# A GEGLU feed-forward block on one core: warm-up matmuls, a new order of the first loads, and eight PSUM banks shared out anew

## The chip, the core and the metric

The kernel runs on one core of a Trainium2 chip. The metric is the device time of one execution in microseconds (us); the time before is the median of five runs.

## What is computed

```python
B, S, D, F = 32, 32, 1024, 3584          # x: B x S x D, weights D x F, D x F, F x D, all bf16

def _gelu(x):
    return jax.nn.gelu(x, approximate=True)

def reference(x, w_gate, w_up, w_down):
    return (_gelu(x @ w_gate) * (x @ w_up)) @ w_down
```

With 32 x 32 = 1024 rows of x, the two projections into F and the one back take 448 matmuls of 128 x 128 weights by 512 columns each, 1344 in all.

## The kernel before

All of x is held transposed in `xT` (128 partitions, DK = 8 slices of D, 1024 columns of tokens). It is filled by two DMA transposes at line 72, one for each block of 512 tokens (`tb` = 0, 1). All of the intermediate result lies in `GT` and all of `w_down` in `Wd`.

**First phase** (lines 91 to 141). An outer loop over seven groups `g` of 512 columns of F loads a tile `wg` of `w_gate` and a tile `wu` of `w_up`, 1 MB each, from a pool of two buffers (so the next group's load can go out while this one is used). In group 0 each of the two loads is split: columns 0 to 127 first (line 79), the other 384 after that (line 82). Behind them comes a chunk of `Wd` (line 97). Inside, for each of the two token blocks and each of four sub-blocks `fsub` of 128 columns, eight matmuls accumulate into a PSUM tile `pg` (line 108), eight into `pu` (line 117), and an element-wise chain follows: Square on ACT (line 125, out `s2`, which the profile calls `s`), a multiply-add on DVE (`inner`, line 127), Sigmoid on ACT (`sg`, line 136), and two multiplies on DVE (`t1`, shown as `t`, line 138; and `GT`, line 139, which is the only step that reads `pu`).

**Second phase** (lines 150 to 165). For each of 16 output tiles 28 matmuls accumulate into `po` (line 154); ACT copies it to SBUF (line 162), and SP sends it out (line 163).

PSUM has eight banks, and each of these tiles takes one: `pg` has three buffers, `pu` three, `po` two. PE, ACT, DVE and SP each run their own instructions in program order; a tile scheduler sets that order and the semaphores. All DMAs are issued by SP's queue, so a transfer that stands later in that queue is issued after the descriptors of all before it have been generated.

Of the kernel before, what the change touches and what calls it, by code (L numbers as in the profile page):

```python
# [1 line left out]

# [4 lines left out]


@with_exitstack  # L10
def kernel(
    ctx: ExitStack,
    tc: tile.TileContext,
    x: bass.AP,
    w_gate: bass.AP,
    w_up: bass.AP,
    w_down: bass.AP,
    out: bass.AP,
):
    nc = tc.nc  # L20
    P = nc.NUM_PARTITIONS

    bf16 = mybir.dt.bfloat16
    f32 = mybir.dt.float32
    ACT = mybir.ActivationFunctionType
    ALU = mybir.AluOpType

    xf = x.flatten_outer_dims()
    of = out.flatten_outer_dims()
    T, D = xf.shape  # L30
    D2, F = w_gate.shape
    assert D2 == D and w_up.shape == (D, F) and w_down.shape == (F, D)
    assert T % P == 0 and D % P == 0 and F % P == 0

    NB = 512
    DK = D // P
    FK = F // P
    TB = T // NB
    DN = D // NB
    TI = T // P  # L40
    FG = NB
    assert F % FG == 0 and T % NB == 0 and D % NB == 0
    NFG = F // FG
    FSUB = FG // P

    k_cubic = 0.044715
    sqrt_k = k_cubic**0.5
    sig_scale = 2.0 * (2.0 / 3.141592653589793) ** 0.5

    wg_v = w_gate.rearrange("(dk p) f -> p dk f", p=P)  # L50
    wu_v = w_up.rearrange("(dk p) f -> p dk f", p=P)
    wd_v = w_down.rearrange("(fk p) d -> p fk d", p=P)

    const_pool = ctx.enter_context(tc.tile_pool(name="consts", bufs=1))
    w_pool = ctx.enter_context(tc.tile_pool(name="wpool", bufs=2))
    work_pool = ctx.enter_context(tc.tile_pool(name="work", bufs=3))
    o_pool = ctx.enter_context(tc.tile_pool(name="opool", bufs=3))
    psum1_pool = ctx.enter_context(tc.tile_pool(name="psum1", bufs=3, space=bass.MemoryType.PSUM))
    psum2_pool = ctx.enter_context(tc.tile_pool(name="psum2", bufs=2, space=bass.MemoryType.PSUM))

    hwdge = [nc.sync, nc.sync]
    ldeng = nc.sync

    xT = const_pool.tile([P, DK, T], bf16, name="xT")
    GT = const_pool.tile([P, FK, T], bf16, name="GT")
    Wd = const_pool.tile([P, FK, D], bf16, name="Wd")
    WD_CHUNK = 4
    assert FK % WD_CHUNK == 0
    NWDC = FK // WD_CHUNK

    for tb in range(TB):
        nc.sync.dma_start_transpose(  # L72
            out=xT[:, :, tb * NB : (tb + 1) * NB],
            in_=xf[tb * NB : (tb + 1) * NB, :],
        )

    def load_w(tile_ap, dram_view, g, split_first):
        if split_first:
            ldeng.dma_start(
                out=tile_ap[:, :, 0:P], in_=dram_view[:, :, g * FG : g * FG + P]  # L80
            )
            ldeng.dma_start(
                out=tile_ap[:, :, P:FG],
                in_=dram_view[:, :, g * FG + P : (g + 1) * FG],
            )
        else:
            ldeng.dma_start(out=tile_ap, in_=dram_view[:, :, g * FG : (g + 1) * FG])

    wd_loaded = [False] * NWDC

    for g in range(NFG):
        wg = w_pool.tile([P, DK, FG], bf16, name="wg")
        load_w(wg, wg_v, g, split_first=(g == 0))
        wu = w_pool.tile([P, DK, FG], bf16, name="wu")
        load_w(wu, wu_v, g, split_first=(g == 0))
        if g < NWDC:
            ldeng.dma_start(
                out=Wd[:, g * WD_CHUNK : (g + 1) * WD_CHUNK, :],
                in_=wd_v[:, g * WD_CHUNK : (g + 1) * WD_CHUNK, :],
            )  # L100
            wd_loaded[g] = True
        for tb in range(TB):
            tsl = slice(tb * NB, (tb + 1) * NB)
            for fsub in range(FSUB):
                fi = g * FSUB + fsub
                pg = psum1_pool.tile([P, NB], f32, name="pg")
                for dk in range(DK):
                    nc.tensor.matmul(  # L108
                        pg,
                        lhsT=wg[:, dk, fsub * P : (fsub + 1) * P],  # L110
                        rhs=xT[:, dk, tsl],
                        start=(dk == 0),
                        stop=(dk == DK - 1),
                    )
                pu = psum1_pool.tile([P, NB], f32, name="pu")
                for dk in range(DK):
                    nc.tensor.matmul(  # L117
                        pu,
                        lhsT=wu[:, dk, fsub * P : (fsub + 1) * P],
                        rhs=xT[:, dk, tsl],  # L120
                        start=(dk == 0),
                        stop=(dk == DK - 1),
                    )
                s2 = work_pool.tile([P, NB], f32, name="s2")
                nc.scalar.activation(s2, pg, ACT.Square, scale=sqrt_k)  # L125
                inner = work_pool.tile([P, NB], f32, name="inner")
                nc.vector.scalar_tensor_tensor(  # L127
                    out=inner,
                    in0=s2,
                    scalar=1.0,  # L130
                    in1=pg,
                    op0=ALU.add,
                    op1=ALU.mult,
                )
                sg = work_pool.tile([P, NB], f32, name="sg")
                nc.scalar.activation(sg, inner, ACT.Sigmoid, scale=sig_scale)  # L136
                t1 = work_pool.tile([P, NB], f32, name="t1")
                nc.vector.tensor_tensor(out=t1, in0=sg, in1=pg, op=ALU.mult)  # L138
                nc.vector.tensor_tensor(  # L139
                    out=GT[:, fi, tsl], in0=t1, in1=pu, op=ALU.mult  # L140
                )

    for c in range(NWDC):
        if not wd_loaded[c]:
            ldeng.dma_start(
                out=Wd[:, c * WD_CHUNK : (c + 1) * WD_CHUNK, :],
                in_=wd_v[:, c * WD_CHUNK : (c + 1) * WD_CHUNK, :],
            )

    for ti in range(TI):  # L150
        for dn in range(DN):
            po = psum2_pool.tile([P, NB], f32, name="po")
            for fk in range(FK):
                nc.tensor.matmul(  # L154
                    po,
                    lhsT=GT[:, fk, ti * P : (ti + 1) * P],
                    rhs=Wd[:, fk, dn * NB : (dn + 1) * NB],
                    start=(fk == 0),
                    stop=(fk == FK - 1),
                )  # L160
            o_sb = o_pool.tile([P, NB], bf16, name="o_sb")
            nc.scalar.activation(o_sb, po, ACT.Copy)  # L162
            nc.sync.dma_start(
                out=of[ti * P : (ti + 1) * P, dn * NB : (dn + 1) * NB], in_=o_sb
            )


# [1 line left out]
_INS = ['x', 'w_gate', 'w_up', 'w_down']  # L169
_OUTS = [((32, 32, 1024), 'bfloat16')]  # L170


# [23 lines left out]
```

## Time and profile before

| | us |
|---|---|
| median of five runs (310.3 to 311.23) | 310.96 |
| the profiled execution's own time | 311.1 |
| its span, first to last instruction | 309.3 |
| PE busy | 291.6 (94%) |
| DVE busy | 115.6 (37%) |
| ACT busy | 80.8 (26%) |

The span is 1.8 us shorter than the time of the same execution; the rest lies around the first and last instruction. PE is shown busy from the first matmul to the last, but its records overlap (matmuls are pipelined and their ends are modelled), so the pace of the matmuls is read from the distance of their starts and not from their length. PEld is the weight load that runs beside the matmuls.

### The profile page before, as it was taken

Reading aid. Unit: us, or ns where it says so; the run is one execution under the profiler, and the core shown is the slowest. Engines: PE = TensorE matmul, PEld = TensorE weight load, DVE = VectorE, ACT = ScalarE, POOL = GpSimd, SP = SyncE. Lnnn points to the kernel's source line nnn. Section 1 sums busy time; section 2 is a strip of 40 time slices with the busy share of each in tenths; the row PEclk is TensorE's granted clock in tenths of the full one; section 3 lists DMA queues with packets and bytes.
Section 4 is the critical chain, followed back from the end, with each engine's and each line's share of the span. In section 5 each row is a group of like instructions: output and inputs, shape, how many; then the busy total and the mean of one; then the engine's idle time right before and its main releaser. Section 6 shows DMA issues by size and latency. Waiting matters only on the chain.

```text
span 309.3 us, 3191 instructions
## 1 busy us (share of the span) xinstructions
PE 291.6 (94%) x1318; PEld 131.9 (43%) x1344; DVE 115.6 (37%) x168; ACT 80.8 (26%) x130; POOL 0.2 (0%) x4
## 2 busy tenths in 40 slices
PE   0399999999999999999999999999999999999995
PEld 0144444444444444444444444444444444444442
DVE  0036655665556565656565656652000000000000
ACT  1043333333333333333333333331000100100010
POOL 0000000000000000000000000000000000000000
PEclk9999999999999999999999999999999999999999
DMA  8999967008002500710170000000100000010000
GB/s 180 260 346 367 388 224 271 2 0 268 5 3 83 188 2 0 234 37 2 27 244 0 2 1 0 2 0 0 34 19 17 29 23 17 17 34 19 18 18 33
DMA packets 30910, 26.41 MB, mean 85 GB/s; under 512 B 10928, under 2 KB 27312, under 8 KB 30896
## 3 DMA queue, kind: packets, MB, share of 16 engines
q1 hardware_dynamic: 30896, 26.22, 26.9%
q8 instruction: 10, 0.16, 0.2%
q14 instruction: 4, 0.03, 0.0%
HBM read 22.02 MB, written 2.10 MB: 78 GB/s over the span
## 4 chain that ended last, share of the span: by engine, by line
PE 94%; SPq 3%; DMA 1%; issue 1%; ACT 0%; ACTq 0%
PE pg L108 32%; PE pu L117 31%; PE po L154 31%; SPq L72 3%; DMA wg<-in_w_gate_dram 1%; ACT o_sb L162 0%; ACTq L162 0%
## 5 line engine op out<-in xcount | busy, mean ns | idle before, releaser
L108 PE MATMUL pg<-xT,wg 128*128 128x512 bf16 x439 | 107.2, 385 | 13.5 <-DMA wg<-in_w_gate_dram 13.1
L117 PE MATMUL pu<-xT,wu 128*128 128x512 bf16 x440 | 105.8, 381 | 0.4
L154 PE MATMUL po<-Wd,GT 128*128 128x512 bf16 x439 | 96.4, 379 | 0.5
L108 PEld LDWEIGHTS <-wg 128*128 128x128 bf16 x448 | 44.1, 99 | 67.0 <-DMA wg<-in_w_gate_dram 13.1
L117 PEld LDWEIGHTS <-wu 128*128 128x128 bf16 x448 | 44.0, 98 | 53.7 <-issue 1.1
L154 PEld LDWEIGHTS <-GT 128*128 128x128 bf16 x448 | 43.8, 98 | 52.9
L125 ACT ACTIVATE s<-pg 128x512 f32<-128x512 f32 x56 | 33.4, 597 | 96.3 <-PE pg L108 93.3
L127 DVE SCALAR_TENSOR_TENSOR inner<-s,pg 128x512 f32<-128x512 f32 x56 | 38.5, 688 | 50.3 <-ACT s L125 50.3
L138 DVE TENSOR_TENSOR t<-sg,pg 128x512 f32<-128x512 f32 x56 | 38.6, 689 | 39.5 <-ACT sg L136 39.5
L136 ACT ACTIVATE sg<-inner 128x512 f32<-128x512 f32 x56 | 35.3, 630 | 41.5 <-DVE inner L127 41.4
L139 DVE TENSOR_TENSOR GT<-t,pu 128x512 bf16<-128x512 f32 x56 | 38.5, 687 | 5.8
L162 ACT ACTIVATE o_sb<-po 128x512 bf16<-128x512 f32 x16 | 9.6, 597 | 87.5 <-PE po L154 87.5
L125 ACT ACT_TABLE_LOAD x1 | 1.3, 1283 | 0.7 <-PEq L180 0.7
L136 ACT ACT_TABLE_LOAD x1 | 1.3, 1283 | 0.0
L180 POOL MEMSET const-bfloat16-1.0<- 128x1 bf16 x1 | 0.1, 101 | 0.0
L180 POOL MEMSET const-uint8-127<- 128x1 uint8 x1 | 0.1, 101 | 0.0
L180 POOL MEMSET const-float32-0.0<- 128x1 f32 x1 | 0.1, 98 | 0.2 <-issue 0.2
L180 POOL MEMSET const-float32-1.0<- 128x1 f32 x1 | 0.1, 98 | 0.0
## 6 DMA issues: line engine op xcount, KB each, us to landing
Wd<-in_w_down_dram SPq DMA_DIRECT2D x7, 1024.0 KB, 12.3
wg<-in_w_gate_dram SPq DMA_DIRECT2D x6, 1024.0 KB, 5.3
wu<-in_w_up_dram SPq DMA_DIRECT2D x6, 1024.0 KB, 7.2
out_dram<-o_sb SPq DMA_DIRECT2D x16, 128.0 KB, 1.7
wg<-in_w_gate_dram SPq DMA_DIRECT2D x1, 768.0 KB, 5.7
wu<-in_w_up_dram SPq DMA_DIRECT2D x1, 768.0 KB, 7.6
wg<-in_w_gate_dram SPq DMA_DIRECT2D x1, 256.0 KB, 3.8
wu<-in_w_up_dram SPq DMA_DIRECT2D x1, 256.0 KB, 6.2
```

Source lines behind the costliest of these rows:

```text
L72: nc.sync.dma_start_transpose(out=xT[:, :, tb * NB : (tb + 1) * NB], in_=xf[tb * NB : (tb + 1) * NB, :],)
L108: nc.tensor.matmul(pg, lhsT=wg[:, dk, fsub * P : (fsub + 1) * P], rhs=xT[:, dk, tsl], start=(dk == 0), stop=(dk == DK - 1),)
L117: nc.tensor.matmul(pu, lhsT=wu[:, dk, fsub * P : (fsub + 1) * P], rhs=xT[:, dk, tsl], start=(dk == 0), stop=(dk == DK - 1),)
L125: nc.scalar.activation(s2, pg, ACT.Square, scale=sqrt_k)
L127: nc.vector.scalar_tensor_tensor(out=inner, in0=s2, scalar=1.0, in1=pg, op0=ALU.add, op1=ALU.mult,)
L136: nc.scalar.activation(sg, inner, ACT.Sigmoid, scale=sig_scale)
L138: nc.vector.tensor_tensor(out=t1, in0=sg, in1=pg, op=ALU.mult)
L139: nc.vector.tensor_tensor(out=GT[:, fi, tsl], in0=t1, in1=pu, op=ALU.mult)
L154: nc.tensor.matmul(po, lhsT=GT[:, fk, ti * P : (ti + 1) * P], rhs=Wd[:, fk, dn * NB : (dn + 1) * NB], start=(fk == 0), stop=(fk == FK - 1),)
L162: nc.scalar.activation(o_sb, po, ACT.Copy)
L180: nc = _bacc.Bacc("TRN2", target_bir_lowering=False, num_devices=1)
```

## The change

Five things change.

1. **Warm-up matmuls.** DVE fills a tile `warm` with zeros, and PE runs 20 matmuls of 128 x 128 by 512 on it ahead of everything else. They write one of the two `po` buffers, and nothing reads the result.
2. **Order of the first loads.** SP issues the transpose of token block 0, then three quarters of the first `wg` (two of the eight D-slices each, all 512 columns), then the whole first `wu`, and then the transpose of token block 1. The first quarter of `wg` is issued by ACT's queue. The splits by columns are gone.
3. **Order of the first matmuls.** In group 0, token block 0, PE goes over D in steps of two slices and, in each step, over all four `fsub`; so 32 `wg` matmuls into four `pg` tiles come ahead of the first `wu` matmul. The four `pu` tiles of this block use both `pu` and both `po` buffers.
4. **PSUM.** One pool: four buffers of `pg`, two of `pu`, two of `po`.
5. **Wd chunks** are asked for from group 1 on, one group later than before.

The function `load_tb0_transposes` is defined and not called. The core of the diff:

```diff
-    psum1_pool = ctx.enter_context(tc.tile_pool(name="psum1", bufs=3, space=bass.MemoryType.PSUM))
-    psum2_pool = ctx.enter_context(tc.tile_pool(name="psum2", bufs=2, space=bass.MemoryType.PSUM))
+    psum_pool = ctx.enter_context(tc.tile_pool(name="psum", bufs=2, space=bass.MemoryType.PSUM))
...
-    for tb in range(TB):
+    def load_tb_transpose(tb):
         nc.sync.dma_start_transpose(
             out=xT[:, :, tb * NB : (tb + 1) * NB],
             in_=xf[tb * NB : (tb + 1) * NB, :],
         )
...
+    warm = const_pool.tile([P, NB], bf16, name="warm")
+    nc.vector.memset(warm, 0.0)
+    pw = psum_pool.tile([P, NB], f32, name="po")
+    for i in range(20):
+        nc.tensor.matmul(pw, lhsT=warm[:, 0:P], rhs=warm, start=True, stop=True)
+
+    for g in range(NFG):
+        if g == 0:
+            load_tb_transpose(0)
+        wg = w_pool.tile([P, DK, FG], bf16, name="wg")
+        if g == 0:
+            for d0 in range(0, DK, 2):
+                (nc.scalar if d0 == 0 else ldeng).dma_start(
+                    out=wg[:, d0 : d0 + 2, :], in_=wg_v[:, d0 : d0 + 2, 0:FG]
+                )
+        else:
+            load_w(wg, wg_v, g)
+        wu = w_pool.tile([P, DK, FG], bf16, name="wu")
+        load_w(wu, wu_v, g)
+        if g == 0:
+            for tb in range(1, TB):
+                load_tb_transpose(tb)
+        if g >= 1:
+            load_wd_chunk(g - 1)
+        for tb in range(TB):
+            tsl = slice(tb * NB, (tb + 1) * NB)
+            if g == 0 and tb == 0:
+                pgs = []
+                for fsub in range(FSUB):
+                    pg = psum_pool.tile([P, NB], f32, name="pg", bufs=FSUB)
+                    pgs.append(pg)
+                for d0 in range(0, DK, 2):
+                    for fsub in range(FSUB):
+                        for dk in range(d0, d0 + 2):
+                            nc.tensor.matmul(
+                                pgs[fsub],
+                                lhsT=wg[:, dk, fsub * P : (fsub + 1) * P],
+                                rhs=xT[:, dk, tsl],
+                                start=(dk == 0),
+                                stop=(dk == DK - 1),
+                            )
+                for fsub in range(FSUB):
+                    pu = psum_pool.tile(
+                        [P, NB], f32, name="pu" if fsub < 2 else "po"
+                    )
+                    up_matmuls(pu, wu, fsub, tsl)
+                    gelu_mul(pgs[fsub], pu, g * FSUB + fsub, tsl)
+            else:
+                for fsub in range(FSUB):
+                    fi = g * FSUB + fsub
+                    pg = psum_pool.tile([P, NB], f32, name="pg", bufs=FSUB)
+                    gate_matmuls(pg, wg, fsub, tsl)
+                    pu = psum_pool.tile([P, NB], f32, name="pu")
+                    up_matmuls(pu, wu, fsub, tsl)
+                    gelu_mul(pg, pu, fi, tsl)
```

`gate_matmuls`, `up_matmuls` and `gelu_mul` hold the same matmuls and the same five element-wise instructions as before.

The rows below are instructions in the order in which an engine's queue holds them: line, operation, output and inputs, shape, and the semaphores waited for. First SP's queue at the start of the program, before (`xT`, `wg`, `wu` and `Wd` are the tiles named above; `DMAHW` with a number is a semaphore that DMA transfers raise as they land).

```order
L72 DMA_TRANSPOSE xT<-in_x_dram 128x8x512 x2
L79 DMA wg<-in_w_gate_dram 128x8x128
L82 DMA wg<-in_w_gate_dram 128x8x384
L79 DMA wu<-in_w_up_dram 128x8x128
L82 DMA wu<-in_w_up_dram 128x8x384
L97 DMA Wd<-in_w_down_dram 128x4x1024
L87 DMA wg<-in_w_gate_dram 128x8x512
L87 DMA wu<-in_w_up_dram 128x8x512 [waits DMAHW0_49]
```

And SP's queue at the same place after the change.

```order
L79 DMA_TRANSPOSE xT<-in_x_dram 128x8x512
L140 DMA wg<-in_w_gate_dram 128x2x512 x3
L85 DMA wu<-in_w_up_dram 128x8x512
L79 DMA_TRANSPOSE xT<-in_x_dram 128x8x512
L85 DMA wg<-in_w_gate_dram 128x8x512
L85 DMA wu<-in_w_up_dram 128x8x512 [waits DMAHW0_49]
L89 DMA Wd<-in_w_down_dram 128x4x1024 [waits DMAHW1_49]
```

The second transpose has moved from the second place in the queue to behind the loads of `wg` and `wu`, the two loads split by columns have become three quarters of `wg` and one whole `wu`, and the first `Wd` chunk now stands behind group 1's `wg` and `wu`.

Now ACT's queue at the start, before (`s` is the output of Square, `sg` that of Sigmoid, `inner` what DVE hands to Sigmoid).

```order
L125 ACT_TABLE_LOAD
L125 ACTIVATE s_103<-pg 128x512 [waits PE_49]
L136 ACT_TABLE_LOAD
L136 ACTIVATE sg<-inner 128x512 [waits DVE_49]
L125 ACTIVATE s_130<-pg 128x512 [waits PE_49]
L136 ACTIVATE sg<-inner 128x512 [waits DVE_49]
```

And ACT's queue at the start after the change.

```order
L140 DMA wg<-in_w_gate_dram 128x2x512
L117 ACT_TABLE_LOAD
L117 ACTIVATE s_150<-pg 128x512 [waits PE_49]
L117 ACTIVATE s_168<-pg 128x512 [waits PE_49]
L117 ACTIVATE s_186<-pg 128x512 [waits PE_49]
L123 ACT_TABLE_LOAD
L123 ACTIVATE sg<-inner 128x512 [waits DVE_49]
L117 ACTIVATE s_204<-pg 128x512 [waits PE_49,Activation_49]
L123 ACTIVATE sg<-inner 128x512 [waits DVE_49] x2
L123 ACTIVATE sg<-inner 128x512 [waits DVE_49,Activation_49]
```

ACT first issues the missing quarter of `wg`, and in the first block three Square instructions now stand ahead of the first Sigmoid, where Square and Sigmoid took turns.

## Rows read from the trace of the kernel before

**Rows 1.** The page's chain that ended last, shares of the span by engine, by line.

```profile
PE 94%; SPq 3%; DMA 1%; issue 1%; ACT 0%; ACTq 0%
PE pg L108 32%; PE pu L117 31%; PE po L154 31%; SPq L72 3%; DMA wg<-in_w_gate_dram 1%; ACT o_sb L162 0%; ACTq L162 0%
```

**Rows 2.** The chain from 0 to 30 us: start, length, what.

```profile
0.73 3.91 SPq L72
...
4.70 4.43 SPq L72
...
9.18 3.85 DMA wg<-in_w_gate_dram
...
13.08 4.45 PE pg L108 x10
```

**Rows 3.** The waits: engine, line, waited for: total us, times, longest.

```profile
PE pg L108 <- DMA wg<-in_w_gate_dram: 13.1, 1, 13.1
```

**Rows 4.** Stages: bounds, length, busy PE PEld DVE ACT POOL (count), clock, DMA share, GB/s.

```profile
0.00:13.08 13.08, 0.00 (x1) 0.01 (x1) 0.00 (x0) 1.28 (x1) 0.20 (x4) 1.00 0.91 202
13.08:21.00 7.92, 7.92 (x25) 2.99 (x26) 2.06 (x3) 2.51 (x3) 0.00 (x0) 1.00 1.11 336
21.00:209.70 188.70, 187.81 (x859) 85.48 (x875) 112.12 (x163) 67.45 (x110) 0.00 (x0) 1.00 0.30 100
209.70:306.10 96.40, 95.88 (x438) 43.41 (x445) 1.38 (x2) 8.97 (x16) 0.00 (x0) 1.00 0.06 21
306.10:309.30 3.20, 0.00 (x0) 0.00 (x0) 0.00 (x0) 0.60 (x1) 0.00 (x0) 0.92 0.12 41
```

**Rows 5.** Timeline, first matmuls' weight loads: start, length, engine, line, operation.

```profile
13.48 0.15 PEld L108 LDWEIGHTS <-wg 128*128 128x128 bf16 x1 [0.28 <-issue]
13.91 0.15 PEld L108 LDWEIGHTS <-wg 128*128 128x128 bf16 x1 [0.28 <-issue]
...
18.60 0.76 PEld L117 LDWEIGHTS <-wu 128*128 128x128 bf16 x4 [0.28 <-issue]
```

**Rows 6.** Timeline, PE alone, from 13 to 30 us.

```profile
20.99 1.89 PE L117 MATMUL pu<-xT,wu 128*128 128x512 bf16 x8
...
24.44 1.89 PE L117 MATMUL pu<-xT,wu 128*128 128x512 bf16 x8
...
27.90 1.89 PE L117 MATMUL pu<-xT,wu 128*128 128x512 bf16 x8
```

**Rows 7.** Timeline, the SP queue's issues.

```profile
9.81 0.57 SPq L82 DMA_DIRECT2D wg<-in_w_gate_dram  x1
...
11.43 1.51 SPq L82 DMA_DIRECT2D wu<-in_w_up_dram  x1
```

**Rows 8.** DMA issues from 0 to 13 us: KB each, us from issue to landing.

```profile
wg<-in_w_gate_dram SPq DMA_DIRECT2D x1, 768.0 KB, 5.7
wu<-in_w_up_dram SPq DMA_DIRECT2D x1, 768.0 KB, 7.6
...
xT<-in_x_dram SPq DMA_TRANSPOSE x2, 6.4
```

**Rows 9.** Windows of 1 us, columns as in group 4.

```profile
2.00:3.00 1.00, 0.00 (x0) 0.00 (x0) 0.00 (x0) 0.01 (x1) 0.00 (x0) 1.00 0.70 157
...
5.00:6.00 1.00, 0.00 (x0) 0.00 (x0) 0.00 (x0) 0.00 (x0) 0.00 (x0) 1.00 1.27 289
```

**Rows 10.** Timeline, one tile's first and last element-wise step.

```profile
21.19 0.60 ACT L125 ACTIVATE s<-pg 128x512 f32<-128x512 f32 x1 [1.95 <-PE pg L108]
...
24.00 0.69 DVE L139 TENSOR_TENSOR GT<-t,pu 128x512 bf16<-128x512 f32 x1
```

**Rows 11.** The page's groups: line, operation, shape, count; busy, mean ns; idle before it, releaser.

```profile
L138 DVE TENSOR_TENSOR t<-sg,pg 128x512 f32<-128x512 f32 x56 | 38.6, 689 | 39.5 <-ACT sg L136 39.5
...
L125 ACT ACT_TABLE_LOAD x1 | 1.3, 1283 | 0.7 <-PEq L180 0.7
...
L180 POOL MEMSET const-float32-0.0<- 128x1 f32 x1 | 0.1, 98 | 0.2 <-issue 0.2
```

More of the change, by code (lines that the diff above doesn't have):

```diff
@@ L57 @@
     o_pool = ctx.enter_context(tc.tile_pool(name="opool", bufs=3))
-    psum1_pool = ctx.enter_context(tc.tile_pool(name="psum1", bufs=3, space=bass.MemoryType.PSUM))
-    psum2_pool = ctx.enter_context(tc.tile_pool(name="psum2", bufs=2, space=bass.MemoryType.PSUM))
-    hwdge = [nc.sync, nc.sync]
+    psum_pool = ctx.enter_context(tc.tile_pool(name="psum", bufs=2, space=bass.MemoryType.PSUM))
     ldeng = nc.sync
@@ L75 @@
         )
[L77 to L141, printed above, removed]
@@ L143, with load_w, load_wd_chunk @@
-    for c in range(NWDC):
-        if not wd_loaded[c]:
+    def load_w(tile_ap, dram_view, g):
+        ldeng.dma_start(out=tile_ap, in_=dram_view[:, :, g * FG : (g + 1) * FG])
+    def load_wd_chunk(c):
+        if c < NWDC and not wd_loaded[c]:
             ldeng.dma_start(
@@ L148, with gate_matmuls, up_matmuls @@
             )
+            wd_loaded[c] = True
+    def gate_matmuls(pg, wg, fsub, tsl):
+        for dk in range(DK):
+            nc.tensor.matmul(
+                pg,
+                lhsT=wg[:, dk, fsub * P : (fsub + 1) * P],
[3 more added lines that the diff above has]
+            )
+    def up_matmuls(pu, wu, fsub, tsl):
+        for dk in range(DK):
+            nc.tensor.matmul(
+                pu,
+                lhsT=wu[:, dk, fsub * P : (fsub + 1) * P],
+                rhs=xT[:, dk, tsl],
+                start=(dk == 0),
+                stop=(dk == DK - 1),
+            )
@@ new lines @@
+    warm = const_pool.tile([P, NB], bf16, name="warm")
[11 more added lines that the diff above has]
+                    out=wg[:, d0 : d0 + 2, :], in_=wg_v[:, d0 : d0 + 2, 0:FG]
+                )
+        else:
[17 more added lines that the diff above has]
+                        for dk in range(d0, d0 + 2):
+                            nc.tensor.matmul(
+                                pgs[fsub],
+                                lhsT=wg[:, dk, fsub * P : (fsub + 1) * P],
+                                rhs=xT[:, dk, tsl],
+                                start=(dk == 0),
+                                stop=(dk == DK - 1),
+                            )
+                for fsub in range(FSUB):
+                    pu = psum_pool.tile(
+                        [P, NB], f32, name="pu" if fsub < 2 else "po"
+                    )
+                    up_matmuls(pu, wu, fsub, tsl)
[8 more added lines that the diff above has]
+                    gelu_mul(pg, pu, fi, tsl)
@@ L150 @@
+    for c in range(NWDC):
+        load_wd_chunk(c)
     for ti in range(TI):
         for dn in range(DN):
-            po = psum2_pool.tile([P, NB], f32, name="po")
+            po = psum_pool.tile([P, NB], f32, name="po")
             for fk in range(FK):
```

19 lines of the change are left out of this document (added).

## The prediction

> **What bounds the kernel now.** I read the chain that ended last first. 94% of it is PE, nearly evenly spread over the three matmul lines, and what is not PE is mainly SP issuing the transposes and a wait for the first `wg` [rows 1]. In order of time [rows 2] SP spends 0.73 to 9.13 on issuing the two transposes, issues the first `wg` columns at 9.18, and these land 3.85 us later; the first matmul starts at 13.08. The waits say the same: PE waits once in the whole program, 13.1 us [rows 3].
>
> Next, how densely PE works from there on. The stages [rows 4] leave only 13.08 us at the start and 3.2 us at the end without matmuls. The granted clock column reads 1.00 throughout, so I read the clock from the matmuls' pace. At first the weight loads, one per matmul, start 0.43 us apart (13.48, 13.91), and this pace holds until a run of fast ones starts at 18.60 [rows 5]: 512 columns in 0.427 us are the 1.2 GHz level. The first matmul starts at 13.08 and (18.6 - 13.08) / 0.427 = 13, so 13 matmuls ran back to back at that level before the clock rose. After that 32 matmuls take 27.90 - 20.99 = 6.91 us [rows 6], 0.216 us each, the 2.4 GHz level. Check: 13.08 + 13 x 0.427 + 1331 x 0.216 = 306.1, where the last stage begins [rows 4]. So in 293 us of PE work there is no gap to speak of. Two things can be saved: the 13.08 us ahead, and 13 x (0.427 - 0.216) = 2.7 us of slow clock.
>
> **The warm-up matmuls.** SP and ACT start at about 0.72 to 0.73 [rows 2], and I take the same for DVE and PE, which show nothing there. The memset covers 128 x 256 words. DVE's nearest row is 0.69 us for 512 elements, and POOL's memset of one element takes 0.1 us [rows 11]; I take half of the first, 0.35, between 0.1 and 0.69. With 0.05 us for the hand-over (9.18 + 3.85 = 13.03 to 13.08 [rows 2]) PE starts at 1.13 (0.88 to 1.47). If zeros raise the clock as data did, 13 matmuls take 5.55 us, to 6.68, and the other 7 take 1.51 us: the warm-up ends at 8.19. From rows alone the ends are 1.13 + 20 x 0.216 = 5.45 with none slow, and 1.13 + 20 x 0.427 = 9.67 with all slow. I take 13, the only count that this trace shows. Beside that row: the Trainium skill (TensorE: Matmul & The Clock Gate, Part 1) says that the number of slow matmuls at the start of one and the same kernel varies between runs, 6, 11 or 14 in its measurement; by an estimate from that the warm-up would end between 6.7 and 8.4 and the time would lie between 302.4 and 303.7.
>
> **When the first operands land.** The first transpose keeps its place: issued at 0.73, landing 6.4 us after its issue [rows 8], at 7.1. Its data flow from a little after 2 us at up to 289 GB/s [rows 9]. New beside it is the quarter of `wg` from ACT's queue, 0.26 MB: at that rate 0.9 us if the transpose stands aside for all of it. So token block 0 is there between 7.1 and 8.0. The Trainium skill (DMA: Bandwidth & Descriptors, Issuing engines are not separate DMA queues) speaks against a gain from the second queue: transfers from all queues interleave on the same 16 engines, and only issue time is saved; that takes the 8.0, which is still ahead of the warm-up's end, and makes 303.3 the lowest time instead of 302.4. The quarter itself: at the soonest 0.73 + 3.85 = 4.6, by the first `wg` load [rows 2]; at the latest, if its descriptors wait for those of the transpose, 4.64 + 3.85 = 8.5. I take it as there before 8.19, being nearer to the row of an idle queue. So PE's first real matmul starts at **8.19**, at the end of the warm-up, with bounds of 7.1 (the transpose) and 9.67.
>
> **Whether PE then runs on.** SP issues the three other quarters from 4.70 on, about 0.57 us each [rows 7]. Before, the second transpose landed at 4.70 + 6.4 = 11.1, all of the first `wg` at 9.81 + 5.7 = 15.5, and all of `wu` at 11.43 + 7.6 = 19.0 [rows 7, 8]: 4.4 us for 1 MB of `wg`, 1.1 us a quarter, and 3.5 us for `wu`. Behind a transpose that lands at 8.0 the quarters are there at 9.1, 10.2 and 11.3, and `wu` at 14.8. Each quarter feeds 8 matmuls, 1.73 us, so they are wanted at 9.9, 11.6 and 13.4, and `wu` after 32 matmuls at 15.1. The margins are 0.8, 1.4, 2.1 and 0.3 us; that order of matmuls, all four `pg` ahead of `pu`, is what hides `wu`, and with the old order `wu` would be wanted after 8 matmuls. The second transpose is issued behind `wu` and lands about 4.1 us after it (11.1 - 7.1 [rows 2, 8]), near 19; it is wanted after 64 matmuls, at 22.0. `Wd`, a group later, is wanted only in the second phase, from 209.7 on [rows 4], and its seven chunks of 1 MB take 25 us at the 3.5 us of `wu`.
>
> The element-wise chain of the first block runs late: ACT has three Squares (0.60 [rows 10]) and a table load (1.28 [rows 11]) ahead of the first Sigmoid. The first `pg` is complete at about 13.9; 13.9 + 1.8 + 1.3 + 0.63 gives the Sigmoid at 17.6, the multiply that frees this `pg` at 18.4, and the first `GT`, which frees the first `pu`, at about 20.4, since DVE does another multiply first. The second block wants that `pg` at 22.0 and that `pu` at 23.7. The margin is over 3 us, so this costs nothing. In steady state a tile's `pu` is written from 20.99 on [rows 6] and its `GT` ends at 24.69 [rows 10]; with two `pu` buffers the next but one `pu` starts 6.91 us after the first, at 27.90. The margin is 3.2 us; nothing.
>
> **Sum.** The start moves from 13.08 to 8.19, -4.9; 13 matmuls at the fast pace, -2.7; nothing else on the path; the 3.2 us at the end stay. Span 309.3 - 7.6 = 301.7. The profiled execution took 311.1, 1.8 more than its span, so it gives 303.5; against the median of 310.96 it gives 303.3. I say **303.4**.
>
> **Rivals.**
> *The zeros don't raise the clock.* No row shows matmuls on zeros. Then the warm-up takes 20 x 0.427 us, to 9.67, and 13 slow matmuls follow as before: only 13.08 - 9.67 = 3.4 us is gained, 307.6. Against it: 13 back-to-back matmuls are all that went before the rise in rows 5. 7 in 100.
>
> *Operands late.* With the quarter from ACT at 8.5 the start slips by 0.3; the later quarters and `wu` then come near or past their times (a 1 MB load at the slower 4.4 us costs another 0.6): 304.4. With the transpose slowed to 10 by the traffic beside it, 305.3; and should the clock fall in that idle time, up to 2.7 more, 308.0. For it are the margins of 0.3 and 0.8 us; against it, that both transposes landed 6.4 us after their issue [rows 8], the second with loads of `wg` and `wu` already issued behind it (from 9.18 on [rows 2], it landed at 11.1). If the reordering did nothing at all and PE started at 13.08 with a fast clock, 308.4 would be left. 14 in 100, mostly between 304 and 306.
>
> *Slower: `pu` with two buffers.* The place is the matmul that opens a `pu` and waits for `GT` two tiles earlier. With L from the start of `pu` to the end of `GT`, two tiles take L where L is over 6.91 us, and some 26 pairs of tiles follow the first block. It decides from L = 7.2 on, when 26 x 0.29 eats the 7.6 us; at 7.5 it would be 303.4 + 15.3 = 318.7. The Trainium skill (Perfetto Trace Analysis, Optimization Strategy) says that a gap that repeats on the engine that should be saturated can mean too little PSUM for the next tile. Rows 6 and 10 give L = 3.70 before, and DVE has work for 3 x 0.69 of every 3.45 us [rows 11], so a backlog from the first block shrinks. 3 in 100.
>
> **Numbers.** Forecast 75 in 100, itself between 302.4 (start at 7.1) and 304.2 (a warm-up from 1.47 on with 15 slow matmuls, to 8.95); late operands 14, no clock gain 7, slower 3, no difference 1. The range takes in the forecast and most of the late operands: 302.2 to 305.9. A measurement of this kernel can tell about 0.2%, 0.6 us, from no change; all cases but the last two are faster by more: faster 0.96, same 0.01, slower 0.03.
>
> **What would show it.** Right: PE at work from about 1.1; weight loads of the warm-up 0.43 us apart until about 6.7, then 0.216; the first `pg` matmul between 7.1 and 8.5, already at the fast pace; no PE wait above 0.3 us on `wg`, `wu`, `xT` or DVE afterwards; last matmul near 298.5. Wrong: slow matmuls on `pg`; a PE wait on the transpose or on `wu` of a microsecond; PE waiting for `GT` in every tile; an end of more than 3.2 us after the last matmul.

## The result

The changed kernel takes 304.01 us, the median of nine runs (302.86 to 304.2), against 310.45 us before in sixteen (309.87 to 311.43): a ratio of 0.9785 with a 95% interval of 0.9771 to 0.9799. That is 6.4 us less, and inside the range of the prediction, 0.6 us above its number. The profiled execution took 303.72 us with a span of 301.9 us.

The page's chain that ended last, of the changed kernel, by engine and by line, answers to [rows 1]:

```profile
PE 98%; issue 1%; ACT 0%; DVE 0%; ACTq 0%
PE po L191 32%; PE pu L107 31%; PE pg L97 30%; PE po L132 2%; PE pg L162 2%; PE po L107 1%; ACT o_sb L199 0%; DVE warm L129 0%; ACTq L199 0%
```

SP's transposes and the wait for `wg` have left the chain; the warm-up (`po` L132, 2%) stands in their place. The stages (bounds, length, busy time of PE, PEld, DVE, ACT, POOL with counts, clock, DMA share, GB/s), as [rows 4]:

```profile
0.00:1.18 1.18, 0.00 (x0) 0.00 (x1) 0.27 (x1) 0.00 (x1) 0.20 (x4) 1.00 0.00 0
1.18:8.35 7.17, 7.17 (x21) 2.69 (x22) 0.00 (x0) 1.28 (x1) 0.00 (x0) 1.00 0.99 230
8.35:22.16 13.81, 13.76 (x64) 6.24 (x64) 6.02 (x10) 5.29 (x9) 0.00 (x0) 1.00 1.08 278
...
298.70:301.90 3.20, 0.00 (x0) 0.00 (x0) 0.00 (x0) 0.57 (x1) 0.00 (x0) 1.00 0.12 41
```

PE is idle for 1.18 us at the start instead of 13.08, and for the same 3.20 us at the end. The timeline of the first 24 us (start, length, engine, line, operation), to be read beside [rows 5, 6, 7]:

```profile
0.73 4.66 SPq L79 DMA_TRANSPOSE xT<-in_x_dram  x1
0.73 0.42 ACTq L140 DMA_DIRECT2D wg<-in_w_gate_dram  x1
0.85 0.27 DVE L129 MEMSET warm<- 128x256 uint32 x1 [0.85 <-PEq L217]
...
1.58 0.15 PEld L132 LDWEIGHTS <-warm 128*128 128x128 bf16 x1 [0.28 <-issue]
...
5.45 1.58 SPq L140 DMA_DIRECT2D wg<-in_w_gate_dram  x3
...
6.70 0.15 PEld L132 LDWEIGHTS <-warm 128*128 128x128 bf16 x1 [0.28 <-issue]
7.05 0.96 PEld L132 LDWEIGHTS <-warm 128*128 128x128 bf16 x5 [0.20 <-issue]
7.08 0.47 SPq L85 DMA_DIRECT2D wu<-in_w_up_dram  x1
...
8.35 7.07 PE L162 MATMUL pg<-xT,wg 128*128 128x512 bf16 x31
...
15.26 3.62 PE L107 MATMUL pu<-xT,wu 128*128 128x512 bf16 x16
...
17.71 0.69 DVE L125 TENSOR_TENSOR t<-sg,pg 128x512 f32<-128x512 f32 x1 [1.04 <-ACT sg L123]
...
19.32 1.28 DVE L126 TENSOR_TENSOR GT<-t,pu 128x512 bf16<-128x512 f32 x2
...
22.16 1.89 PE L97 MATMUL pg<-xT,wg 128*128 128x512 bf16 x8
...
23.89 1.67 PE L107 MATMUL pu<-xT,wu 128*128 128x512 bf16 x7
```

The zeros are written at 0.85 in 0.27 us. The weight loads of the warm-up are 0.43 us apart up to 6.70, and faster from 7.05 on: 13 matmuls at 1.2 GHz, on zeros, a fourteenth of 0.35 us in which the clock rises, and then the 2.4 GHz level. The first real matmul starts at 8.35, right behind the warm-up; 32 matmuls later (the row shows 31, one record is missing), at 15.26, the first `wu` matmul, and another 32 later, at 22.16, the second token block, each 6.9 us on: no gap. From there to the end of PE's work, at 298.70, 1280 matmuls take 276.54 us, 0.216 us each, so no gap is left in the steady state either. The landings (KB each, us from issue to landing; issues from 0 to 5 us, then from 7 to 14 us), as [rows 8]:

```profile
wg<-in_w_gate_dram ACTq DMA_DIRECT2D x1, 256.0 KB, 3.1
xT<-in_x_dram SPq DMA_TRANSPOSE x1, 6.8
```

```profile
wu<-in_w_up_dram SPq DMA_DIRECT2D x1, 1024.0 KB, 7.7
...
xT<-in_x_dram SPq DMA_TRANSPOSE x1, 10.9
```

So ACT's quarter of `wg` lands at 3.8, the first transpose at 0.73 + 6.8 = 7.5, `wu` at 7.08 + 7.7 = 14.8 (0.46 us before it is wanted), and the second transpose at 18.5.

### The profile page after: what moved, and what is told of

The parts are those of the page before. It is cut to its first block, busy times and chain, and to the rows that moved or that the text cites. A ratio compares the mean times of both kernels' runs of the same rounds, so it can differ in the third digit from the quotient of the medians.

```text
span 301.9 us, 3230 instructions
## 1 busy us (share of the span) xinstructions
PE 296.0 (98%) x1337; PEld 133.9 (44%) x1364; DVE 115.2 (38%) x169; ACT 80.3 (27%) x130; POOL 0.2 (0%) x4
## 4 chain that ended last, share of the span: by engine, by line
PE 98%; issue 1%; ACT 0%; DVE 0%; ACTq 0%
PE po L191 32%; PE pu L107 31%; PE pg L97 30%; PE po L132 2%; PE pg L162 2%; PE po L107 1%; ACT o_sb L199 0%; DVE warm L129 0%; ACTq L199 0%
## 5 line engine op out<-in xcount | busy, mean ns | idle before, releaser
L107 PE MATMUL pu<-xT,wu 128*128 128x512 bf16 x423 | 100.9, 379 | 0.4
L97 PE MATMUL pg<-xT,wg 128*128 128x512 bf16 x408 | 97.5, 379 | 0.5
L126 DVE TENSOR_TENSOR GT<-t,pu 128x512 bf16<-128x512 f32 x54 | 37.0, 687 | 5.4
L132 PE MATMUL po<-warm 128*128 128x512 bf16 x20 | 7.3, 551 | 1.2 <-DVE warm L129 1.2
L162 PE MATMUL pg<-xT,wg 128*128 128x512 bf16 x31 | 7.0, 379 | 0.1
L132 PEld LDWEIGHTS <-warm 128*128 128x128 bf16 x20 | 2.6, 134 | 5.4 <-issue 3.8
L107 PE MATMUL po<-xT,wu 128*128 128x512 bf16 x16 | 3.6, 379 | 0.0
L126 DVE TENSOR_TENSOR GT<-t,po 128x512 bf16<-128x512 f32 x2 | 1.4, 684 | 0.1
```

The source lines that it names most:

```text
L97: nc.tensor.matmul(pg, lhsT=wg[:, dk, fsub * P : (fsub + 1) * P], rhs=xT[:, dk, tsl], start=(dk == 0), stop=(dk == DK - 1),)
L107: nc.tensor.matmul(pu, lhsT=wu[:, dk, fsub * P : (fsub + 1) * P], rhs=xT[:, dk, tsl], start=(dk == 0), stop=(dk == DK - 1),)
L126: nc.vector.tensor_tensor(out=GT[:, fi, tsl], in0=t1, in1=pu, op=ALU.mult)
L132: nc.tensor.matmul(pw, lhsT=warm[:, 0:P], rhs=warm, start=True, stop=True)
L162: nc.tensor.matmul(pgs[fsub], lhsT=wg[:, dk, fsub * P : (fsub + 1) * P], rhs=xT[:, dk, tsl], start=(dk == 0), stop=(dk == DK - 1),)
```

## The experiments

Each time is a median beside runs of the kernel before on the same chip (310.48 to 310.8).

### The parts of the change

**The changed kernel without its warm-up.**

```diff
-    warm = const_pool.tile([P, NB], bf16, name="warm")
-    nc.vector.memset(warm, 0.0)
-    pw = psum_pool.tile([P, NB], f32, name="po")
-    for i in range(20):
-        nc.tensor.matmul(pw, lhsT=warm[:, 0:P], rhs=warm, start=True, stop=True)
```

> The changed kernel without its 20 warm-up matmuls. My theory: the warm-up is worth only what it hides of the slow clock, less what it delays the first real matmul. Without it PE starts when the first transpose has landed (0.73 + 6.8 = 7.5 in the trace after) instead of at 8.35, and 13 or 14 real matmuls run at 0.427 instead of 0.216 us: -0.8 + 2.8 = +2.0, so 305.9 to 306.1 against 304.0. Rival, that the early loads depend on nothing but their order and the warm-up is worth the whole slow stretch or more: 306.8 or later. Rival, that the first real matmuls are fast without it: 303.2.

Measured: 305.5 us (305.07 to 306.12), ratio 0.9839 (0.9817 to 0.9862). Its wait on the transpose (engine, line, waited for: total us, times, longest) and two weight loads of the first real matmuls:

```profile
PE pg L157 <- DMA xT<-in_x_dram: 7.6, 1, 7.6
```

```profile
8.01 0.15 PEld L157 LDWEIGHTS <-wg 128*128 128x128 bf16 x1 [0.28 <-issue]
...
11.42 4.67 PEld L157 LDWEIGHTS <-wg 128*128 128x128 bf16 x22 [0.28 <-issue]
```

PE starts at 7.62, and the loads are 0.43 us apart until 11.42: (11.42 - 7.62) / 0.427 = 9 real matmuls at 1.2 GHz, where I had expected 13 or 14. By the medians the warm-up is worth 1.5 us (305.5 - 304.01), less than the 2.0 that the theory gave. In the profiled execution the form of the sum holds and the count was off: a start 0.73 us sooner and 9 x 0.211 = 1.9 us of slow clock make 1.2, the difference of the spans (303.1 and 301.9).

**The kernel before with the warm-up and nothing else.**

```diff
+    warm = const_pool.tile([P, NB], bf16, name="warm")
+    nc.vector.memset(warm, 0.0)
+    pw = psum2_pool.tile([P, NB], f32, name="po")
+    for i in range(20):
+        nc.tensor.matmul(pw, lhsT=warm[:, 0:P], rhs=warm, start=True, stop=True)
```

> The kernel before with nothing but the 20 warm-up matmuls. They end near 8.2, and PE then stands idle until the first weights land at 13.1, 4.9 us. If the clock, once up, lasts over this idle time, the first real matmuls run at 0.216 us and 2.7 us are gained: 307.7. If it falls, the first 13 run at 0.427 again and nothing is gained: 310.4. I expect it to fall, or to fall after some matmuls: 309 to 310.5.

Measured: 310.47 us (309.53 to 311.29), ratio 0.9999 (0.9982 to 1.0017): nothing. The wait, and the weight loads on both sides of it:

```profile
PE pg L114 <- DMA wg<-in_w_gate_dram: 5.7, 1, 5.7
```

```profile
4.14 0.15 PEld L95 LDWEIGHTS <-warm 128*128 128x128 bf16 x1 [0.28 <-issue]
4.45 2.26 PEld L95 LDWEIGHTS <-warm 128*128 128x128 bf16 x11 [0.16 <-issue]
...
13.26 0.15 PEld L114 LDWEIGHTS <-wg 128*128 128x128 bf16 x1 [0.28 <-issue]
...
17.53 0.15 PEld L123 LDWEIGHTS <-wu 128*128 128x128 bf16 x1 [0.28 <-issue]
17.95 0.98 PEld L123 LDWEIGHTS <-wu 128*128 128x128 bf16 x5 [0.27 <-issue]
```

A stretch of the same execution, columns as in [rows 4]:

```profile
12.00:17.95 5.95, 5.09 (x12) 1.80 (x13) 0.69 (x1) 1.44 (x2) 0.00 (x0) 0.50 1.13 318
```

The zeros raise the clock here too, after 7 or 8 matmuls (from 4.45 on the loads are 0.2 us apart). Then PE stands idle for 5.65 us, and from 12.86 on the first 12 real matmuls run at 0.43 us again, until 17.95: the clock had fallen. Its granted column shows it: 1.00 from PE's last warm-up matmul to 11.00, 0.50 from 11.25 on and until 17.95. Nine of the ten executions have a mean granted clock of 0.988 to 0.994, below every run of the kernel before (0.998 to 1.000), so the fall is the rule; the tenth, at 1.000, took 309.53 us, and no profile shows it. Here a warm-up that ended 5.65 us before the operands landed bought nothing.

**The changed kernel with the first block in the order of the others.**

```diff
-            if g == 0 and tb == 0:
+            if False:
```

> The changed kernel with the first block in the old order of matmuls (eight wg, eight wu, for each of the four sub-blocks). My theory: this order wants wu after 8 matmuls, when it has not landed. In the trace after, the last quarter of wg lands at 11.0 and wu at 14.8; PE has then done 8 matmuls where the new order has done 30, so 22 x 0.216 = 4.8 us are lost: 308.8, with one PE wait on wu of over 3 us; up to 2.7 more if the clock falls in it. Rival, that wu's landing is not what matters and the order is worth nothing: 304.0.

Measured: 306.58 us (305.99 to 308.57), ratio 0.9884 (0.9846 to 0.9922). PE's timeline:

```profile
7.79 0.59 PE L97 MATMUL pg<-xT,wg 128*128 128x512 bf16 x2
9.36 1.30 PE L97 MATMUL pg<-xT,wg 128*128 128x512 bf16 x4 [0.97 <-DMA wg<-in_w_gate_dram]
12.40 4.88 PE L97 MATMUL pg<-xT,wg 128*128 128x512 bf16 x14 [1.74 <-DMA wg<-in_w_gate_dram]
17.12 3.62 PE L107 MATMUL pu<-xT,wu 128*128 128x512 bf16 x16
```

Only part of the 4.8 us that I expected is there, because the scheduler did not keep the order as written: it put 20 `wg` matmuls (all of two sub-blocks and half of a third) ahead of the first `wu` one. The rows show other waits instead: on the quarters of `wg`, 0.97 and 1.74 us, since the first sub-block wants all four of them in a row. This profile is of the slowest of the four executions (308.57; the others took 305.99 to 306.75). In it the clock fell behind these waits: 14 matmuls from 12.40 take 4.88 us, where 14 at the 2.4 GHz level take 3.2. The granted clock reads 1.00 through both waits and until 12.60, and 0.50 from 12.70 on, so it fell only once PE had taken up work again:

```profile
12.40:16.00 3.60, 3.60 (x10) 1.28 (x10) 0.69 (x1) 0.60 (x1) 0.00 (x0) 0.54 1.23 200
```

The mean granted clock of this execution is 0.994 and that of the other three 1.000: in those it did not fall, so what they lose has another cause; the waits are the one that this profile shows.

**The same without the warm-up**, so that the new order of loads is left, with the PSUM split and the later `Wd` chunks:

```diff
-    warm = const_pool.tile([P, NB], bf16, name="warm")
-    nc.vector.memset(warm, 0.0)
-    pw = psum_pool.tile([P, NB], f32, name="po")
-    for i in range(20):
-        nc.tensor.matmul(pw, lhsT=warm[:, 0:P], rhs=warm, start=True, stop=True)
...
-            if g == 0 and tb == 0:
+            if False:
```

> The changed kernel without its warm-up and with the first block left to the scheduler, so that mainly the new order of loads (and the PSUM split) is left of the change. In the run with the warm-up and this block order, PE waited for the last quarter of wg until 12.4 and the clock had fallen by then, so the warm-up had bought nothing there. My theory: without the warm-up the time is the same as that run's 306.6 within 0.6. If the warm-up was worth its 1.6 us there too (as it was with the new block order): 308.2.

Measured: 307.83 us (306.49 to 308.0), ratio 0.9897 (0.9873 to 0.9922). My theory, 306.6, was wrong in the median; the other, 308.2, is nearer, though two of the six runs took some 306.5 and four some 307.9; what parts them is open. PE's timeline of one of the four (307.94):

```profile
7.68 1.01 PE L97 MATMUL pg<-xT,wg 128*128 128x512 bf16 x2 [7.68 <-DMA xT<-in_x_dram]
8.95 4.60 PE L97 MATMUL pg<-xT,wg 128*128 128x512 bf16 x15 [0.25 <-DMA wg<-in_w_gate_dram]
16.01 3.63 PE L107 MATMUL pu<-xT,wu 128*128 128x512 bf16 x16 [2.47 <-DMA wu<-in_w_up_dram]
```

PE starts on the first slices at 7.68, is through with all that it can do without `wu` at 13.5, and waits 2.47 us for `wu`, which lands 8.75 us after its issue at 7.22 in this run, at 15.97. So in this execution it is `wu` that costs, and this order has less work to put ahead of it.

Each median against the kernel before in its own set gives the steps: order of loads, -3.0; with the order of the first block, -5.1; with the warm-up as well, -6.4 (-6.7 in the second set, below). So the steps are about 3.0, 2.1 and 1.4 to 1.7 us, the first two no firmer than the two groups of runs of the version with the loads only. In the other order the warm-up brings 1.0 (306.58 is 4.0 below its kernel before) and the block order 2.4 to 2.7. The order of loads and of the first block bring three quarters of the gain or more, and the warm-up alone none. The PSUM split and the later `Wd` chunks are in the first step, and no run parts them from the loads; the matmuls of the steady state follow each other every 0.216 us before and after, so there they give and take nothing.

### The rival that would have made it slower

**One `pu` buffer instead of two.**

```diff
-                        [P, NB], f32, name="pu" if fsub < 2 else "po"
+                        [P, NB], f32, name="po" if fsub in (1, 2) else "pu",
+                        bufs=2 if fsub in (1, 2) else 1,
...
-                    pu = psum_pool.tile([P, NB], f32, name="pu")
+                    pu = psum_pool.tile([P, NB], f32, name="pu", bufs=1)
```

> The changed kernel with one pu buffer instead of two (in the first block the last sub-block takes it again; seven banks are used). It tests the mechanism that two buffers leave unseen. From the trace before, GT ends 3.5 us after its pg is complete; with one buffer a pu waits for the GT of the tile ahead, and since pg runs in between, two tiles take 3.62 + 3.59 = 7.21 us instead of 6.91: 0.15 us for each of 52 tiles, +7.8 us, 311 to 312. The cruder form that I used in the prediction (one tile takes all of L = 3.75 us) gives 0.3 x 52 = +15.6 us, 319.6. If PE does not wait for GT at all: 304.0.

Measured: 312.57 us (312.36 to 313.44), ratio 1.0075 (1.0049 to 1.0101), 8.6 us slower than the changed kernel, and a little more than the 311 to 312 that I expected. Tiles of the steady state, and the wait by number:

```profile
62.39 0.69 DVE L126 TENSOR_TENSOR GT<-t,pu 128x512 bf16<-128x512 f32 x1
...
63.13 1.89 PE L107 MATMUL pu<-xT,wu 128*128 128x512 bf16 x8
...
65.94 0.69 DVE L126 TENSOR_TENSOR GT<-t,pu 128x512 bf16<-128x512 f32 x1
...
66.68 1.89 PE L107 MATMUL pu<-xT,wu 128*128 128x512 bf16 x8
...
70.38 1.89 PE L107 MATMUL pu<-xT,wu 128*128 128x512 bf16 x8
```

```profile
PEld L107 <- issue: 15.3, 52, 0.4
```

Each `pu` starts just behind the end of the `GT` of the tile ahead (62.39 + 0.69 = 63.08, then 63.13; 65.94 + 0.69 = 66.63, then 66.68). Starts are 3.55 and 3.70 us apart in turn, 7.25 for two tiles against 6.91; over 26 pairs that is 8.8 us. The view puts the 52 waits down to "issue" and not to DVE, so they are found by the times of `GT` and `pu`. The mechanism of the rival is real and near: one bank fewer, and the change would be a loss. With two buffers the margin holds: the changed kernel's 0.216 us per matmul from 22.16 to 298.70 leaves no room for such a wait.

### What bounds the start now

The next four ran on one chip: the changed kernel again, fewer warm-up matmuls, the first quarter on SP, and a version meant to be faster.

**The changed kernel again.**

> The changed kernel again, beside the three that follow, so that they can be compared on one chip: 304.0, its own median so far.

Measured: 303.75 us (303.44 to 304.91), ratio 0.9803 (0.9778 to 0.9828). PE's waits:

```profile
PE pg L162 <- DMA xT<-in_x_dram: 0.6, 1, 0.6
...
PE pu L107 <- DMA wu<-in_w_up_dram: 0.2, 1, 0.2
```

In this execution only 6 warm-up matmuls were slow, and PE had to wait 0.57 us for the transpose, to 7.53, and 0.20 us for `wu`. In the first profile of this kernel 13 were slow and a fourteenth in part, and neither wait is there. The span differs by 0.4 us only (301.5 and 301.9).

**16 warm-up matmuls** (`range(16)` for `range(20)`).

> The changed kernel with 16 warm-up matmuls instead of 20. The last four cost 4 x 0.216 = 0.86 us, and the first transpose lands at 7.5, so the first real matmul starts at 7.5 instead of 8.35. My theory: wu then becomes the bound, since 32 matmuls after 7.5 it is wanted at 14.4 and it lands at 14.8, so about half of the gain is lost in a wait of 0.4 us: 303.5, and a PE wait on wu. If the warm-up alone sets the pace: 303.1. If the transpose or something else sets the start already: 304.0.

Measured: 303.56 us (303.44 to 303.81), ratio 0.9782 (0.9762 to 0.9802). PE's waits:

```profile
PE pg L162 <- DMA xT<-in_x_dram: 1.0, 1, 1.0
...
PE pu L107 <- DMA wu<-in_w_up_dram: 0.4, 1, 0.4
```

As the theory had it: the transpose sets the start (7.67) and `wu` takes back 0.40 us. That the time is lower than with 20 is not shown: 303.56 lies within the changed kernel's own runs (302.86 to 304.91).

**The first quarter of `wg` on SP.**

```diff
-                (nc.scalar if d0 == 0 else ldeng).dma_start(
+                ldeng.dma_start(
```

> The changed kernel with the first quarter of wg issued by SP, behind the transpose, instead of by ACT. SP is free at 5.45 and a quarter lands some 3.4 us after its issue, at 8.9, so the first real matmul starts at 8.9 instead of 8.35; the later quarters and wu are issued 0.5 us later, but the transpose is rid of 0.26 MB beside it. 304.5 to 305.0. If the second queue is worth nothing (the same engines carry the same bytes): 304.0.

Measured: 303.58 us (303.32 to 303.87), ratio 0.9782 (0.9762 to 0.9802): the same as with ACT's queue. Its landings (issues from 0 to 5 us):

```profile
wg<-in_w_gate_dram SPq DMA_DIRECT2D x1, 256.0 KB, 3.5
xT<-in_x_dram SPq DMA_TRANSPOSE x1, 5.9
```

Without ACT's quarter beside it the transpose lands 5.9 us after its issue instead of 6.8, and SP is done with issuing it after 3.77 us instead of 4.66; the quarter, issued at 4.56, is there at 8.06, before the warm-up ends. I had SP free at 5.45, as in the trace with ACT's quarter, and that is why I expected a loss.

**The first transpose in halves, two quarters on ACT, 10 warm-up matmuls.**

```diff
-            load_tb_transpose(0)
+            load_tb0_transposes()
...
-                (nc.scalar if d0 == 0 else ldeng).dma_start(
+                (nc.scalar if d0 <= 2 else ldeng).dma_start(
...
-    for i in range(20):
+    for i in range(10):
```

> A version meant to beat the changed kernel: the transpose of token block 0 in two halves of D (the function that the changed kernel defines and does not call), two quarters of wg on ACT's queue, and 10 warm-up matmuls. If half a transpose lands near 5, the first real matmul starts at 5.5, at the end of the warm-up, and the rest of the slow stretch (about 4 matmuls) is spent on real work: 2.9 - 0.9 = 2.0 us gained less a wait for wu of about 0.6: 302.3 to 302.8. If two halves cost as much as a whole before the first lands, or the loads on ACT's queue push the transposes back: 304.0 or later.

Measured: 303.69 us (303.5 to 304.05), ratio 0.9787 (0.9766 to 0.9807): no gain. PE's waits:

```profile
PE pg L162 <- DMA xT<-in_x_dram: 1.9, 1, 1.9
...
PE pu L107 <- DMA wu<-in_w_up_dram: 0.8, 1, 0.8
```

The first half lands at 6.98 and not near 5, and what that gives, `wu` takes back: 0.79 us. The four versions of this set start between 6.98 and 8.27 and yet their spans lie between 301.5 and 301.8; in the three that start before 8 us PE waits for `wu`, to between 14.79 and 15.14. So `wu` has become the next bound, just behind the warm-up.

**`wu` of group 0 in two halves of columns, 16 warm-up matmuls.**

```diff
-        load_w(wu, wu_v, g)
+        if g == 0:
+            for c0 in (0, FG // 2):
+                ldeng.dma_start(
+                    out=wu[:, :, c0 : c0 + FG // 2],
+                    in_=wu_v[:, :, c0 : c0 + FG // 2],
+                )
+        else:
+            load_w(wu, wu_v, g)
...
-    for i in range(20):
+    for i in range(16):
```

> The changed kernel with 16 warm-up matmuls and the first wu load cut into two halves of 256 columns. In all four variants of the last job PE started between 6.98 and 8.27, and yet their spans lay within 0.3 us; in three of them PE waited for wu, which landed at 14.8 to 15.1. My theory: wu's landing is the floor. The first two sub-blocks need only its first half, which should land about 1.7 us earlier, so PE runs on from the landing of the transpose at 7.6: 7.6 + 1344 x 0.216 + 3.2 = 301.1 span, 302.9, 0.5 to 0.8 below the changed kernel. If wu is not the floor, or rows of 512 B are slower by as much: 303.6 or more.

Measured: 303.28 us (303.23 to 303.56), ratio 0.9768 (0.9746 to 0.9789). Its one PE wait on a transfer:

```profile
PE pg L169 <- DMA xT<-in_x_dram: 1.2, 1, 1.2
```

The wait on `wu` is gone, as the theory said, but the transpose landed later in this execution, at 7.9 instead of 7.5, and the span is 301.6: 303.28 and not the 302.9 that I expected. Why the transpose landed later is open.

**With the halves of the transpose and 12 warm-up matmuls as well**, one quarter on ACT:

> The run before this one with, in addition, the first transpose in two halves of D and 12 warm-up matmuls, one quarter of wg on ACT's queue. With two halves and two quarters on ACT's queue the first half landed at 7.0, when the last job ran it, and a whole transpose beside one quarter at 7.5. Theory: first matmul at 6.5 to 7.0, wu's first half wanted at 13.4 to 13.9 and there at about 13.2, with a few slow matmuls left in runs where the clock rises late: 302.2 to 302.6. If two half transposes push wu back by as much as they bring x forward: 302.9 or more.

Measured: 303.12 us (302.88 to 303.44), ratio 0.9761 (0.974 to 0.9783), the lowest median of all, and yet above the 302.2 to 302.6 of the theory. PE's waits on transfers:

```profile
PE pg L169 <- DMA wg<-in_w_gate_dram: 1.6, 1, 1.6
...
PE pg L169 <- DMA xT<-in_x_dram: 0.6, 1, 0.6
```

PE starts at 5.88 now, and waits 1.59 us for the second quarter of `wg`. Each bound that is moved uncovers the next one. These two versions have lower ratios than the changed kernel (0.9785 and 0.9803 in its two sets of runs), but the intervals overlap; that they are faster is not settled.

## Why the prediction was right, point by point

**The start of the warm-up.** Predicted 1.13, measured 1.18. The memset took 0.27 us, not 0.35, and DVE began at 0.85, not 0.73.

**Do zeros raise the clock?** The step that no row of the kernel before showed, and right: the first rival, 307.6, falls with the weight loads at 6.70 and 7.05. The count was 13 slow matmuls and a part, against the 13 taken from [rows 5]. That this was luck shows in the nine other profiles that begin with the same warm-up: by the spacing of the weight loads they had 6, 6, 7, 7, 7, 9, 9, 11 and 13 wholly slow ones, and one of those with 6 is the changed kernel itself. It does little harm, since the transpose then sets the start; this is the floor that the prediction had at 7.1 to 8.0. The trace agrees with the sentence of the Trainium skill (TensorE: Matmul & The Clock Gate, Part 1) that the number of slow matmuls at the start of one kernel varies between runs (6, 11 or 14 in its measurement): the changed kernel had 13 and a part in one profile and 6 in the other. The prediction read the granted clock as 1.00 throughout; [rows 4] show 0.92 in the last 3.20 us, where no matmul runs, so nothing hung on it.

**The start of the real work.** Predicted 8.19, measured 8.35, the end of the warm-up in both.

**The transpose.** Predicted 7.1 to 8.0, measured 7.5 with ACT's quarter and 6.6 without it. The 0.9 us between them is the number that was worked out, but it is one profile against another: with the quarter the whole transpose landed 6.7 to 7.2 us after its issue in eight profiles, without it 5.9 in the run with the quarter on SP and 6.2 to 6.5 in the two kernels with the old loads. By bytes the transpose stood aside, as assumed (0.78 MB had moved by 5 us with the quarter on ACT, 0.77 with it on SP), and SP's issue of it took the same 0.9 us longer; which of the two sets the landing no run tells. The sentence of the Trainium skill (DMA: Bandwidth & Descriptors, Issuing engines are not separate DMA queues) agrees: by 5 us the two queues together had moved no more, and the kernel without the second measures the same (303.58 and 303.75 us).

**The loads behind it.** `wu` at 14.8 in both; margin 0.3 predicted, 0.46 measured. The step from which this came was off: SP issued the quarters from 5.45 on and not from 4.70, because the transpose took 4.66 us to issue. They landed sooner after their issue, and the two errors cancel. The margin was as thin as stated: with a start 0.7 to 0.8 us sooner, `wu` is late by 0.20 to 0.40 us.

**The chain of ACT and DVE.** The multiply that frees the first `pg` ends at 17.71 + 0.69 = 18.40, just as worked out, and the first two `GT` by 20.60, the first of them before the 20.4 of the prediction; the buffers are wanted at 22.16 and 23.89, so the margins are over 3 us.

**The rival that ends slower.** The place was right, as the run with one buffer shows, and the size was not: by the form in the prediction each tile would lose all that its chain is longer than 3.45 us. But a tile that waits has its `pg` complete before its `pu` starts, so its chain is already under way, and the longer the wait, the sooner the chain ends behind that start (3.55 and 3.70 us from one `pu` to the next in turn). Two tiles together lose 0.34 us, about what the form gave to one. One buffer costs 8.6 us, where the form, carried over to one buffer, gives 15.6.

**The sum.** Start 13.08 - 8.35 = 4.7 us instead of 4.9, slow clock 13 x 0.211 = 2.7 us: 7.4, and the span fell by 7.4 (309.3 to 301.9). The medians moved by 6.4. The profile of before was of one of the slower executions (311.1, where sixteen now give 310.45), that of the changed kernel of one of its faster (303.72, median 304.01): 0.65 + 0.29 us make up that difference. Whether the slower executions are those with more slow matmuls no profile tells, so that 13 was the right number to save in the median is not shown; a version without the warm-up had 9. Of the 0.6 us by which the prediction was low, 0.2 lie in the profiled execution (303.5 predicted), 0.3 between that and the median after, and 0.1 are what the prediction took off for the median before.

## What to carry to other kernels

Look for what the first matmul waits for, issue only that first, and order the first block so that it uses each piece as it lands; here that is worth some 5.1 of 6.4 us. See that real work follows warm-up matmuls closely: here the same 20 gave 1.5 us where it followed at once and nothing where 5.65 us of idle time lay between. Before a buffer is taken away, compare the time from its first write to its last read with the time until it comes round again; here two buffers left 3.2 us and one cost 8.6 us in all.

## What the runs showed of the hardware

The number of slow matmuls at the start of a program, all with the same warm-up instructions, was 6 to 13 and a part from one profile to the next. Before the first rise the granted clock column reads 1.00 although the pace is 0.43 us per matmul (the changed kernel from 1.18 to 6.70), so there only the pace tells the level; after a fall the column shows it (0.50 from 12.00 to 17.95 in the kernel before with the warm-up, beside the same pace). Once up, the clock lasted over waits of 1.89 us (the version with halves and 10 warm-up matmuls) and 2.47 us (the one with the loads only), and was down after 5.65 us; and in one execution it fell 0.2 to 0.3 us after PE had taken up work again at 12.40, behind two waits of 0.97 and 1.74 us with four matmuls between them. Half of a transpose did not land in half the time: PE starts on the first half 5.15 us after its issue in one version (5.88 - 0.73) and 6.25 us in the other (6.98 - 0.73), against a landing after 5.9 to 7.2 us for a whole one.
